# Strided sparse attention and an ELU layer pair: the order of the whole run written out as one list of small steps

## The chip, the cores and the metric

The kernel runs on one core of one Trainium2 chip. The metric is the device time of one execution in microseconds (us). The kernel before takes 330.32 us, the median of three runs (329.69 to 331.02).

Engines are named as in the profile: PE does matmuls, PEld is its loading of weights, DVE is VectorE, ACT is ScalarE, POOL is GpSimd, and SP is the sync engine, which here only issues DMAs. PSUM is eight banks of 128 x 512 fp32 that PE writes and DVE and ACT read.

## What is computed

Eight batches of eight heads, 576 rows of 64. Heads 0 to 3 look at the last 32 positions (local), heads 4 to 7 at all earlier positions with the same remainder by 32 (strided). The result, 4608 tokens of 512, goes through two weight matrices with an ELU between.

```python
scores = scale * np.matmul(q, k.transpose(0, 1, 3, 2))
mask_local = (rel >= 0) & (rel < stride)
mask_strided = (rel >= 0) & (pos[None, :] % stride == pos[:, None] % stride)
...
attn = attn / (np.sum(attn, axis=-1, keepdims=True) + 1e-09)
return np.matmul(attn, v).astype(np.float32)
...
h = x @ w_in
g = np.where(h > 0.0, h, alpha * (np.exp(np.minimum(h, 0.0)) - 1.0))
return (g @ w_out).astype(np.float32)
```

## The kernel before

**Tiling.** Each batch is four head pairs, called s0, s1 (strided) and l0, l1 (local). A pair's queries and keys are transposed so that the 64 features lie on partitions (lines 354 and 368 on PE for the early batches, lines 212 and 217 by DMA from SP for later ones: strided from batch 3, local from batch 4). Scores of keys by queries go to PSUM (line 451; line 479 for batch 0), ACT takes the exp (460 and 462; 488), DVE multiplies by a mask of zeros and ones (465; 495). Then PE multiplies by v, which has a column of ones for the denominator (515), DVE takes the reciprocal and normalises (522, 523) into x, PE transposes x (550, 563), and ACT or DVE copies it into xT (557, 559, 567), features by tokens. The local heads also need v of the 32 rows before each block, the halo (413).

**The two layers.** Tokens are taken in nine chunks of 512. For each of 16 column blocks of the first layer, `moe_in` does four matmuls (595), ACT takes exp (616), DVE computes min(e, 1) - 1 (623) and the max of that and h (625). For five blocks of the first chunk, ACT takes the Relu (619) and one DVE instruction does the rest (620). `moe_out` does a quarter of an output group of 128 tokens, four matmuls (635); after the fourth, ACT copies the bank out (639) and SP stores it (641).

**Order.** Nothing is scheduled by a tool: each engine runs its instructions in the order of the program. Batch 0 follows the list `OPENING`. From then on a loop over chunks alternates one `moe_in` of chunk nb with one `moe_out` of chunk nb - 1; in the 32 gaps between them stand pieces of the attention of batch nb + 1, at places set by `TIMES` (a start, a pitch from pair to pair, and the offset of each piece). A piece is coarse: `transposes` is the matmuls and the copy, `av` the matmuls and the normalisation, `scores_all` the scores of both halves of a pair, three exps and two masks.

**Banks.** A pair of neighbouring banks, `pair_a`, takes most of the scores of a pair; two single banks take the rest. Batch 0 has a second pair, `pair_b`, whose two banks serve the first layer later. The other single banks go round in small rings (`Ring`, `share`) for the first layer, the output groups, and everything else.

**Loads.** All loads of q, k, v and weights are DMAs from POOL, which cast fp32 to bf16, in the order of the program; only q of batch 0 is loaded as fp32 from SP and cast by ACT and DVE (341). Batch nb + 3 is loaded while chunk nb is computed, and the DMA transposes of batch nb + 2 are issued by `transpose_batch` at the seventh column block of chunk nb.

Of the kernel before, what the change touches and what calls it, by code (L numbers as in the profile page):

```python
# [10 lines left out]
F32 = mybir.dt.float32  # L11
# [7 lines left out]
STRIDE = 32  # L19
# [13 lines left out]
PIECES = (-2, -1, 0, 2, 3, 5, 7, 0)  # L33
TIMES = (
    None,
    (4, 6, (-3, -2, 0, 2, 4, 6, 9, 3)),
    (6, 6, (-3, -2, 0, 2, 4, 6, 8, 0)),
    (2, 7, PIECES),
)

OPENING = """
s0.cast_q s0.t_q s0.t_k s1.cast_q s1.t_k s0.s0 s1.t_q s0.s1 l0.t_q s1.s1 s1.s0 l0.t_k
l1.t_q l0.s0 s0.v l1.t_k s1.a0 s0.a0 l0.s1 s1.a1 s0.a1 l1.s0 l1.s1 s1.x s0.x s1.halo
l0.a0 l0.a1 l1.a0 l1.a1 l0.x moe.2 l1.x moe.3 moe.0 moe.1
""".split()
ON_VECTOR = "s0.t_q s1.cast_q s1.t_k l0.t_q s0.v l1.x".split()

MERGED = 1


ON_SCALAR = (4, 7, 10, 13, 15)
AHEAD = 3
# [3 lines left out]
def kernel(  # L59
# [24 lines left out]
    p_raw = inner.enter_context(tc.tile_pool(name="raw", bufs=2))  # L84
    p_p = inner.enter_context(tc.tile_pool(name="probs", bufs=3))
    p_x = inner.enter_context(tc.tile_pool(name="x", bufs=2))
    p_g = inner.enter_context(tc.tile_pool(name="g", bufs=2))


    ps = inner.enter_context(tc.tile_pool(name="ps", bufs=1, space=PSUM))  # L90
    pair_a = ps.tile([128, 2, 512], F32, tag="pair_a")
    singles = [ps.tile([128, 512], F32, tag=f"single{i}", name=f"single{i}")
               for i in range(4)]

    used = []

    class Ring:
        def __init__(self, *banks):
            self.banks = banks

        def next(self):

            for bank in self.banks:
                if all(bank is not u for u in used):
                    break
            else:
                bank = next(u for u in used if any(u is b for b in self.banks))
                used[:] = [u for u in used if u is not bank]
            used.append(bank)
            return bank  # L110


    rings = {}

    def share(sc, hps, ops, ring):
        rings.update(sc=Ring(*sc), hps=Ring(*hps), ops=Ring(*ops), ring=Ring(*ring))


    opening = ctx.enter_context(ExitStack())
    p_p0 = opening.enter_context(tc.tile_pool(name="probs0", bufs=8))  # L120
    p_k = opening.enter_context(tc.tile_pool(name="keys", bufs=1))
    ps_open = ctx.enter_context(ExitStack())
    ps_b = ps_open.enter_context(tc.tile_pool(name="ps_b", bufs=1, space=PSUM))
    pair_b = ps_b.tile([128, 2, 512], F32, tag="pair_b")

    def bf16_bank():
        return rings["ring"].next().bitcast(BF16)
# [11 lines left out]
    v_loc = [consts.tile([128, 4, 6, D + 1], BF16, tag=f"v_loc{i}", name=f"v_loc{i}")  # L139
             for i in range(3)]  # L140
    v_str = [consts.tile([128, 4, 5, D + 1], BF16, tag=f"v_str{i}", name=f"v_str{i}")
             for i in range(3)]

    def several(n, name, *shape):
        return [consts.tile([128, *shape], BF16, tag=f"{name}{i}", name=f"{name}{i}")
                for i in range(n)]
# [3 lines left out]
    nat = {(n, kind): several(3, f"{n}_{kind}", w * D)  # L150
           for n in "qk" for kind, w in (("str", 20), ("loc", 4 * L_RUN))}

    qT = {"str": several(2, "qT_str", 10, 128), "loc": several(2, "qT_loc", 2, 640)}
    kT = {"str": several(2, "kT_str", 10, 128), "loc": several(2, "kT_loc", 2, 32 + 640)}


# [5 lines left out]
    raw = {}  # L162
    src = {"q": q, "k": k, "v": v}

    def load_strided(b, name, engine=nc.gpsimd, heads=range(4)):
        rows = src[name][b, 4:8].rearrange("h (t r) d -> h t r d", r=STRIDE)
        if b == 0 and name in stage:
            t = stage[name]
        elif name == "v":
            if b not in raw:  # L170
                raw[b] = p_raw.tile([128, 4, 5, D], BF16, tag="v_raw", name="v_raw")
            t = raw[b]
        else:
            t = nat[name, "str"][b % 3].rearrange("p (h g d) -> p h g d", h=4, d=D)
        for h in heads:
# [32 lines left out]
    def transpose_batch(b):  # L208

        if b >= BY_DMA:  # L210
            for name, to in (("q", qT), ("k", kT)):
                nc.sync.dma_start_transpose(out=to["str"][b % 2],
                                            in_=nat[name, "str"][b % 3])
        if b >= EARLY:
            for name, to, o in (("q", qT, 0), ("k", kT, 32)):
                for a in range(2):
                    nc.sync.dma_start_transpose(
                        out=to["loc"][b % 2][:, a, o:o + 640].rearrange(
                            "p (i r) -> p i r", r=128),
                        in_=nat[name, "loc"][b % 3][:, 640 * a:640 * a + 640])  # L220

    def load_batch(b):
        for name in "qkv":
            load_strided(b, name)
        for name in "qkv":
            load_local(b, name)

# [16 lines left out]
    def clear_v(i, engine=nc.vector):  # L244
# [5 lines left out]
    share([pair_a, pair_b], [], [], singles[:3])  # L250
    warm = consts.tile([1, 1], F32, tag="warm")
    stage = {n: p_g.tile([128, 4, 5, D], F32, tag="g_sb", name=f"{n}_stage")
             for n in "q"}
# [10 lines left out]
    key_i = p_k.tile([128, 126], I32, tag="key_i")  # L264
# [4 lines left out]
    key_q = p_k.tile([128, 126], BF16, tag="key_q")  # L269
    nc.vector.tensor_copy(key_q, key_i)  # L270
    key_ps = bf16_bank()
    nc.tensor.transpose(key_ps[0:126, 0:126], key_q[0:126, :], identity[0:126, 0:126])
    diff = p_k.tile([128, 126], F32, tag="diff")
    same = p_k.tile([128, 126], F32, tag="same")
# [8 lines left out]
    for g in range(3):  # L283
        c = 252 + 108 * g
        nc.vector.tensor_copy(mask_s[0:126, c:c + 108], mask_s[0:126, 0:108])
    clear_v(0)
    nc.vector.memset(kT["loc"][0][:, :, 0:32], 0.0)

    load_strided(0, "k")
    load_local(0, "q")  # L290
    load_local(0, "k")
    load_strided(0, "v")

# [7 lines left out]
    load_local(0, "v")  # L301
# [3 lines left out]

    wi = moe_w_in.rearrange("(c p) f -> p c f", p=128)
    wo = moe_w_out.rearrange("(m p) d -> p m d", p=128)

    def load_w_in(i):
        nc.gpsimd.dma_start(out=w_in_sb[:, :, 512 * i:512 * (i + 1)],  # L310
                            in_=wi[:, :, 512 * i:512 * (i + 1)])

    load_w_in(0)
    load_strided(1, "q")
    load_strided(1, "k")
    load_w_in(1)
    load_strided(1, "v")
    load_local(1, "q")
    load_local(1, "k")
    load_w_in(2)  # L320


    class Pair:
        def __init__(self, b, strided, hp):
# [3 lines left out]
            self.name = f"{self.kind}{hp}"  # L328
            self.pr, self.x = {}, None

        def copy(self, step, late):

            if self.b == 0:
# [559 lines left out]
```

## Time and profile before

| What | us |
|---|---|
| median of three runs | 330.32 |
| profiled execution, its span | 330.3 |
| PE busy | 306.8 (93%) |
| DVE busy | 246.6 (75%) |
| ACT busy | 175.6 (53%) |
| POOL busy | 148.0 (45%) |
| first matmul of the first layer starts | 23.98 |
| first matmul of the second layer starts | 58.46 |
| last matmul ends | 324.70 |

The page of the profile also cuts the span into 40 slices of 8.26 us. Each digit below is the busy share of PE, of DVE and of the 16 DMA engines in tenths:

```
PE   0888778999999999999999999999999999999993
DVE  6583988788788888889889888888888666866500
DMA  6999999999999999999999906310001110010112
```

A busy PE is not PE at its peak: its matmuls overlap, and their ends are modelled. The distance from one start to the next tells the rate.

### The profile page before, as it was taken

The page shows a single profiled execution, that of the slowest core. Times are in us where ns is not written, and L with a number is a line of the kernel's source. Part 1 is how long each engine was busy: PE and PEld are TensorE (multiplying, and loading weights), DVE is VectorE, ACT ScalarE, POOL GpSimd, SP SyncE. Part 2 cuts the span into 40 slices and gives each one's busy share as a digit, 9 for nine tenths or more (in the row PEclk, how much of TensorE's full clock was granted, in tenths as well). Part 3 has the DMA queues.
Part 4 walks back from the last instruction along what each step waited for, and adds up shares of the span by engine and source line. Part 5 has one row for each costly group of instructions (what it writes and reads, how often), then busy time and mean ns, then how long its engine had stood idle before and what let it go on. Part 6 is the DMA issues. An engine that isn't in the chain of part 4 may idle for free.

```text
span 330.3 us, 6240 instructions
## 1 busy us (share of the span) xinstructions
PE 306.8 (93%) x2262; PEld 153.2 (46%) x2262; DVE 246.6 (75%) x540; ACT 175.6 (53%) x344; POOL 148.0 (45%) x233
## 2 busy tenths in 40 slices
PE   0888778999999999999999999999999999999993
PEld 0564444455545554454454444444444444444441
DVE  6583988788788888889889888888888666866500
ACT  3744968667555655554555455545664443444220
POOL 8988666996599479969796100000000000000000
PEclk9999979999999999999999999999999999999999
DMA  6999999999999999999999906310001110010112
GB/s 103 149 138 181 183 207 111 134 141 144 152 124 130 131 190 105 117 143 211 127 125 136 181 34 139 86 50 34 32 35 50 52 45 32 32 37 34 62 66 70
DMA packets 100092, 35.11 MB, mean 106 GB/s; under 512 B 77837, under 2 KB 95445, under 8 KB 100053
## 3 DMA queue, kind: packets, MB, share of 16 engines
q0 software_dynamic: 68016, 18.10, 59.7%
q1 hardware_dynamic: 32037, 16.52, 24.3%
q8 instruction: 20, 0.33, 0.4%
q14 instruction: 19, 0.16, 0.2%
HBM read 36.70 MB, written 9.44 MB: 140 GB/s over the span
## 4 chain that ended last, share of the span: by engine, by line
PE 81%; ACT 5%; DVE 5%; POOL 4%; issue 1%; DMA 1%; ACTq 0%; POOLq 0%
PE single L635 37%; PE half L595 32%; PE single L595 4%; PE single L515 3%; PE pair_a L451 1%; ACT e_sb L616 1%; ACT pr L462 1%; PE single L368 1%; DMA q_str<-in_q_dram 1%; DVE g_sb L625 1%; PE single L563 1%; PE single L550 1%; PE single L451 1%; DVE e_sb L623 1%; POOL v_loc L188 1%
## 5 line engine op out<-in xcount | busy, mean ns | idle before, releaser
L635 PE MATMUL single<-w_out_sb,g_sb 128*128 128x512 bf16 x576 | 145.5, 380 | 0.5
L595 PE MATMUL half<-xT,w_in_sb 128*128 128x512 bf16 x512 | 134.7, 385 | 0.5 <-DVE xT L567 0.5
L616 ACT ACTIVATE e_sb<-half 128x512 f32<-128x512 f32 x128 | 76.9, 600 | 99.8 <-PE half L595 97.0
L623 DVE TENSOR_SCALAR e_sb<-e_sb 128x512 bf16<-128x512 f32 x139 | 64.1, 461 | 44.8 <-ACT e_sb L616 42.7
L625 DVE TENSOR_TENSOR g_sb<-e_sb,half 128x512 bf16<-128x512 bf16 x123 | 84.6, 688 | 4.6
L635 PEld LDWEIGHTS <-g_sb 128*128 128x128 bf16 x576 | 53.5, 98 | 61.7 <-issue 2.5
L595 PEld LDWEIGHTS <-w_in_sb 128*128 128x128 bf16 x576 | 52.9, 100 | 57.0 <-issue 3.9
L639 ACT COPY o_sb<-single 128x512 f32<-128x512 f32 x36 | 21.3, 591 | 19.4 <-PE single L635 19.4
L515 PEld LDWEIGHTS <-pr 128*128 128x128 bf16 (+3 forms) x352 | 20.7, 106 | 16.6 <-issue 2.7
L462 ACT ACTIVATE pr<-pair_a 126x936 bf16<-126x936 f32 (+1 forms) x28 | 27.4, 979 | 0.0
L188 POOL DMA_DIRECT2D v_loc<-in_v_dram x32 | 24.5, 798 | 2.0 <-DMA k_loc<-in_k_dram 1.0
L176 POOL DMA_DIRECT2D k_str<-in_k_dram x32 | 21.2, 707 | 4.3 <-DMA w_out_sb<-in_moe_w_out_dram 2.3
L176 POOL DMA_DIRECT2D v_raw<-in_v_dram x32 | 22.2, 803 | 1.5 <-DMA k_str<-in_k_dram 0.9
L176 POOL DMA_DIRECT2D q_str<-in_q_dram x28 | 18.1, 660 | 10.4 <-DMA k_loc<-in_k_dram 5.2
L595 PE MATMUL single<-xT,w_in_sb 128*128 128x512 bf16 x64 | 18.7, 409 | 0.0
L523 DVE TENSOR_TENSOR x_l<-single,rden 96x384 bf16<-96x384 f32 x32 | 17.7, 553 | 1.1
L523 DVE TENSOR_TENSOR x_s<-single,rden 126x256 bf16<-126x256 f32 (+1 forms) x32 | 15.7, 491 | 1.1
L616 ACT ACTIVATE e_sb<-single 128x512 f32<-128x512 f32 x16 | 9.7, 609 | 11.0 <-PE single L595 11.0
L200 POOL DMA_DIRECT2D q_loc<-in_q_dram x16 | 12.9, 948 | 2.6 <-DMA v_raw<-in_v_dram 0.9
L460 ACT ACTIVATE pr<-single 108x108 bf16<-108x108 f32 (+1 forms) x56 | 11.3, 261 | 4.2 <-PE single L451 4.2
L465 DVE TENSOR_TENSOR pr<-pr,mask_l 128x192 bf16<-128x192 bf16 (+1 forms) x28 | 11.9, 452 | 2.0 <-ACT pr L462 1.9
L200 POOL DMA_DIRECT2D k_loc<-in_k_dram x16 | 12.1, 782 | 2.4 <-DMA q_loc<-in_q_dram 1.9
(106 smaller groups left out, 264.6 us busy)
## 6 DMA issues: line engine op xcount, KB each, us to landing
out_dram<-o_sb SPq DMA_DIRECT2D x36, 256.0 KB, 2.9
v_loc<-in_v_dram POOLq DMA_DIRECT2D x32, 72.0 KB, 5.8
k_str<-in_k_dram POOLq DMA_DIRECT2D x32, 67.5 KB, 4.3
v_raw<-in_v_dram POOLq DMA_DIRECT2D x32, 67.5 KB, 5.2
w_in_sb<-in_moe_w_in_dram POOLq DMA_DIRECT2D x4, 512.0 KB, 6.7
w_out_sb<-in_moe_w_out_dram POOLq DMA_DIRECT2D x4, 512.0 KB, 13.2
q_str<-in_q_dram POOLq DMA_DIRECT2D x28, 67.5 KB, 4.6
q_loc<-in_q_dram POOLq DMA_DIRECT2D x4, 288.0 KB, 5.6
```

The costliest lines, as they stand in the source:

```text
L176: engine.dma_start(out=t[0:108, h].rearrange("p g d -> p (g d)"), in_=rows[h, :, 0:30, :].rearrange("t (r g) d -> t r (g d)", g=5))
L188: nc.gpsimd.dma_start(out=v_loc[b % 3][32:128, h, :, :D], in_=v[b, h].rearrange("(i p) d -> p i d", p=LB))
L200: nc.gpsimd.dma_start(out=t[:, h // 2, 0:4, h % 2], in_=src[name][b, h, 0:512].rearrange("(i p) d -> p i d", p=128))
L462: nc.scalar.activation(main, sc[0:nk, :, 0:w], ACT.Exp, scale=scale)
L515: nc.tensor.matmul(av[0:m, p, blk - b0, :], lhsT=pr[0:nk, o:o + m], rhs=vt[0:nk, 2 * self.hp + p, blk, :], start=True, stop=True)
L523: nc.vector.tensor_tensor(self.x[0:nq, b0:b0 + n].rearrange("q g p d -> q p g d"), av[0:nq, :, 0:n, 0:D], r.unsqueeze(3).to_broadcast([nq, ...
L595: nc.tensor.matmul(hps, lhsT=w_in_sb[:, c, m * 128:(m + 1) * 128], rhs=xT[:, c, nb * N_TILE:(nb + 1) * N_TILE], start=start, stop=stop)
L616: nc.scalar.activation(e_sb, hps, ACT.Exp)
L623: nc.vector.tensor_scalar(e1_sb, e_sb, scalar1=1.0, scalar2=1.0, op0=ALU.min, op1=ALU.subtract)
L625: nc.vector.tensor_tensor(g_of[nb][:, m, :], e1_sb, hps, op=ALU.max)
L635: nc.tensor.matmul(ops, lhsT=g_of[nb][:, m, kk * 128:(kk + 1) * 128], rhs=w_out_sb[:, m, :], start=(m == 0), stop=(m == MC - 1))
L639: nc.scalar.copy(o_sb, ops)
```

## The change

`OPENING`, `PIECES`, `TIMES`, the rings and the loop over chunks are gone. In their place stands one list, `ORDER`, of about 1240 steps, and one loop that deals them out. A step names what is done, the bank or buffer that it uses (after @), and for copies the engine (after /: A is ACT, D is DVE, S a DMA from SP). Its first lines and a stretch from the steady part:

```diff
+ORDER = """
+0s0.cast/D 0s0.tq@1 0s1.cast/D 0s0.cq/A busy.1 0s1.tq@2 0s1.cq/D 0s0.tk@3 0s0.ck/D
+0s1.tk@4 busy.1 0s0.s1@0 0s1.ck/D 0s0.e1@0 0l0.tq@5 0s0.m1 0l1.tq@1 0l0.cq/A 0s1.s1@0
...
+5s1.s0@0 5s0.n1 o3.1.0@5 x4.4@2 5s1.halo 5s1.e0@2 i4.5@4 r4.4/D 5s1.m0 g4.4 5s0.x@6
```

Of a pair, tq and tk are the transposes on PE, cq and ck their copies, s0 and s1 the scores of the two halves, e the exp, m the mask, a the product with v, n the normalisation, x the transposes of x and y their copy, v the copies of strided v, halo the halo. Of the layers, i is an input group (i0.0.2 one matmul of it), x its exp, r the first part of the ELU, g the second, o a quarter of an output group, c its copy and store. What was one piece is now two or three steps that can stand apart.

What changes besides the order:

- **Banks.** One pair (slot 0) takes all scores, one half of a head pair at a time; the other six banks (slots 1 to 6) take everything else, each step naming its own.

```diff
+PAIRS = 1
-        def scores_all(self):
...
+        def s(self, u, copy, slot):
+            self.bank["s" + u] = sc = pairs_ps[slot]
...
+        def e(self, u, copy, slot):
+            if slot is not None:
+                self.pr = pr_sb[slot]
+            t, _, w = self.probs(int(u))
+            nc.scalar.activation(t, self.bank["s" + u][0:t.shape[0], :, 0:w], ACT.Exp,
+                                 scale=scale)
```

  Per head pair there are two exps of about 500 to 650 columns in place of two short and one long.

- **ELU.** The first part is written straight into g and the second works in place. Which column blocks take the Relu on ACT is in the list (r.../A): 11 of chunk 0, 26 of the chunks after it.

```diff
+        elif kind == "r":
+            e, by_scalar = e_of[c, i][0], copy == nc.scalar.copy
+            if by_scalar:
+                nc.scalar.activation(g[:, i, :], h_of[c, i], ACT.Relu)
+            else:
+                nc.vector.tensor_scalar(g[:, i, :], e, scalar1=1.0, scalar2=1.0,
+                                        op0=ALU.min, op1=ALU.subtract)
```

- **Fillers.** `busy(n)` is n matmuls of 512 columns on zeros into the last bank: 3 and 13 before batch 0, and 10 more in the opening of the list.

```diff
+    idle_sb = xT[:, 0, n_tokens - N_TILE:]
+    nc.gpsimd.memset(idle_sb, 0.0)
+
+    def busy(n):
+
+        for _ in range(n):
+            nc.tensor.matmul(singles[-1], lhsT=idle_sb[:, 0:128], rhs=idle_sb,
+                             start=True, stop=True)
```

- **Loads.** The order of POOL's loads up to batch 2 is a list, `LOADS`; local v of batch 0 comes before the selects that make the local mask. Strided v of batches 0 and 1 is loaded as fp32 from SP into the space of the second g buffer, and cast by the copies that place it.

```diff
+    stage = {"q0": staged[:, 0], "v0": staged[:, 1], "v1": staged[:, 1]}
...
+            load_strided(i, name, nc.sync if f"{name}{i}" in stage else nc.gpsimd)
```

- **DMA transposes.** They are steps of the list: turn.3s, turn.4s and turn.4l and so on, strided and local apart. turn.3s stands after c0.3 (the last store of chunk 0) and i2.0:

```diff
+o1.0.0@4 c0.3/A g1.15 2l1.x@1 o1.0.1 2l1.y/D i2.0@6 3s0.v0/D turn.3s 3s0.v1/D i2.1@5
+x2.0@2 i2.2@2 r2.0/D x2.1@0 g2.0 o1.0.2 r2.1/A x2.2@1 g2.1 i2.3@3 r2.2/D o1.0.3 g2.2
+x2.3@2 i2.4@1 r2.3/D c1.0/A g2.3 o1.1.0@6 x2.4@0 3s0.s0@0 r2.4/D i2.5@5 3s0.e0@0
```

The loop that deals the list out:

```diff
+    for token in ORDER:
+        token, _, slot = token.partition("@")
+        slot = int(slot) if slot else None
+        token, _, engine = token.partition("/")
+        copy = {"A": nc.scalar.copy, "S": None}.get(engine, nc.vector.tensor_copy)
+        what, _, rest = token.partition(".")
+        if what in pairs:
+            pairs[what].step(rest, copy, slot)
...
+        elif what == "turn":
+            (transpose_strided if rest[1] == "s" else transpose_local)(int(rest[0]))
+        elif what == "busy":
+            busy(int(rest))
         else:
+            moe(what[0], (what[1:], *rest.split(".")), copy, slot)
```

The numbers of matmuls, transposes, DMA transposes and stores of the computation itself are as before.

More of the change, by code (lines that the diff above doesn't have):

```diff
@@ L83, with several, bank, bank16 @@
     inner = ctx.enter_context(ExitStack())
[L84 to L87, printed above, removed]
+    work = inner.enter_context(tc.tile_pool(name="work", bufs=1))
     ps = inner.enter_context(tc.tile_pool(name="ps", bufs=1, space=PSUM))
[L91 to L127, printed above, removed]
+    def several(pool, n, name, *shape, dtype=BF16):
+        return [pool.tile([128, *shape], dtype, tag=f"{name}{i}", name=f"{name}{i}")
+                for i in range(n)]
+    pairs_ps = several(ps, PAIRS, "pair", 2, 512, dtype=F32)
+    singles = several(ps, 8 - 2 * PAIRS, "single", 512, dtype=F32)
+    def bank(i):
+        return pairs_ps[i][:, 0] if i < PAIRS else singles[i - PAIRS]
+    def bank16(i):
+        return (pairs_ps[i].bitcast(BF16)[:, 0] if i < PAIRS
+                else singles[i - PAIRS].bitcast(BF16))
     w_in_sb = consts.tile([128, KC, d_ff], BF16, tag="w_in_sb")
@@ L304 @@
     nc.vector.memset(kT["loc"][1][:, :, 0:32], 0.0)
[L306 to L320, printed above, removed]
+    for what in LOADS[LOADS.index("w.in.0"):]:
+        load(what)
     class Pair:
@@ L440, in scores_all, with v @@
[L440 to L447 removed]
+        def v(self, part, copy, slot):
+            o = rows_of(v_str[self.b % 3][:, :, :, 0:D], slice(0, 4))[int(part)]
+            copy(o, rows_of(strided_dst(self.b, "v"), slice(0, 4))[int(part)])
@@ L467, in scores_all @@
[L467 to L479 removed]
+                nc.tensor.matmul(sc[:, half, i * nq:(i + 1) * nq],
```

643 lines of the change are left out of this document (310 added, 333 removed).

## The prediction, made before the changed kernel was run

> **What bounds the kernel now.** I read the busy times by stage first, then what PE waits for, then PE's own timeline in the opening. The stages are cut at PE's first transpose of q (7.91), its first input-layer matmul (23.98), the first ELU exp (29.03), the first output-layer matmul (58.46) and PE's last matmul (324.70). Columns: busy us of PE, PEld, DVE, ACT, POOL, then granted clock, DMA, GB/s.
>
> ```profile
> 0.00:7.91 7.91, 0.37 (x2) 0.19 (x2) 5.27 (x24) 2.36 (x5) 6.89 (x18) 1.00 0.60 99
> 7.91:23.98 16.07, 13.35 (x172) 9.78 (x173) 11.28 (x30) 9.65 (x18) 14.55 (x23) 1.00 1.25 146
> 23.98:29.03 5.05, 5.05 (x20) 2.14 (x18) 1.35 (x4) 0.64 (x1) 4.22 (x8) 1.00 1.15 160
> 29.03:58.46 29.43, 22.68 (x237) 12.87 (x236) 24.31 (x52) 24.34 (x49) 20.76 (x32) 0.94 1.24 168
> 58.46:324.70 266.24, 265.31 (x1838) 128.25 (x1836) 204.41 (x432) 137.99 (x271) 101.55 (x157) 1.00 0.79 97
> 324.70:330.30 5.60, 0.01 (x1) 0.00 (x0) 0.00 (x0) 0.59 (x1) 0.00 (x0) 0.95 0.16 54
> ```
>
> From 58.46 on PE is busy 265.31 of 266.24 us and DVE 77%. All waits of PE from 58 to 325 are one line:
>
> ```profile
> PE half L595 <- DVE xT L567: 0.5, 1, 0.5
> ```
>
> So nothing is to be won there except fewer matmuls, and the change removes none; it can only lose there. What can be won lies before 58.46, where no engine is full. There the first twelve input matmuls (two, one, two, one ...) run at half rate:
>
> ```profile
> 27.02 1.06 PE L595 MATMUL half<-xT,w_in_sb 128*128 128x512 bf16 x2
> 27.87 0.63 PE L595 MATMUL single<-xT,w_in_sb 128*128 128x512 bf16 x1
> 28.30 1.06 PE L595 MATMUL half<-xT,w_in_sb 128*128 128x512 bf16 x2
> ...
> 31.65 1.04 PE L595 MATMUL half<-xT,w_in_sb 128*128 128x512 bf16 x4
> ```
>
> Three take 28.30 - 27.02 = 1.28, 0.427 each; at 31.65 four take 0.87 up to the next start (32.52), 0.217 each. The stage costs 5.05 where 12 x 0.215 = 2.6 would do.
>
> **Steady part and tail: 266.24 + 1.1 + 5.60.** The output layer, its copies and the last store are the same steps, so the tail stays 5.60. At the first output matmul the old order has already done one input group of the next chunk (four matmuls from 57.35, 0.86) and the last transposes of batch 1 (0.21); the new list has them still to do: +1.1. Shorter exps on ACT (two of 0.59 to 0.72 a pair for 0.27 + 0.27 + 0.98) and Relus moved to ACT for 26 column blocks after the first chunk's cost nothing, for both engines have room under PE; without that room each Relu would cost 0.61 on ACT.
>
> **Opening to the first input group: 27.1 in place of 29.03.** Two filler groups (3 and 13 matmuls on zeros) run while PE waits for q, from 3.65 to 7.91 in the old trace; sixteen at 0.427 are 6.8, so from about 2 they end near 9 at worst, before the cast below. The casts of q both go to DVE; the second waits for q's last two heads, as in the old trace at 9.69. From there DVE has, up to the last strided copy into xT: casts, q and k copies, eight masks, eight normalisations, the halo, v. At the mean durations of their rows that is 15.5 us. Means overlap: the 52 DVE instructions of the old stage 29.03 to 58.46 have durations that add to 26.7 against 24.31 busy, so 0.91: 14.2. Waits on the way, worked along the list: second half of q, the copy before the second mask, v by SP's queue: 1.6. End 9.7 + 14.2 + 1.6 = 25.5; the first group's first bank is done seven matmuls later, 1.5 warm: 27.0, exp at 27.1. Bounds: 26 (no waits) and 29.5 (one us for v, matmuls at 0.427).
>
> v of batches 0 and 1 leaves POOL's queue for SP's: ten issues of 0.8 less on POOL, which lets the local v and the weights be issued 3 us earlier; on SP they stand behind q's five, which end at 4.87, so the first five end near 9, as they did on POOL (9.70), and share the transfer engines with k. Hence the one us above.
>
> Eight score steps now share one pair of banks, where the opening had two pairs. Each is matmuls 0.25, exp 0.65 and handover 0.1, so 8 x 1.0 = 8 us in a row, inside DVE's 14.2; if DVE were faster, this would be next.
>
> **First exp to the first output matmul: 23 in place of 29.43.** In this stretch the list gives DVE 13 final ELU steps x 0.69, 5 first halves x 0.45, 8 masks (3.6), 7 normalisations (4.9), five copies (2.7), the halo (0.5): 23.0; and ACT 15 exps x 0.60, 9 Relus x 0.61, 8 score exps (5.2), five copies (3.3): 23.0. Times 0.91 each is 20.9. The old order was busy 24.31 of 29.43 on DVE. Walking the list with these durations, DVE and ACT seldom find their next step unready, since scores, ELU blocks and copies alternate; I allow 2 us of waits: 22.9. Bounds: 20.9 (none) and 20.9 x 29.43 / 24.31 = 25.3 (as loose as before). First output matmul: 27.1 + 22.9 = 50.0, bounds 47 to 55. There PE waits 0.3 for the last normalisation of batch 1.
>
> Weights cover this: the output weights' transfers are issued by 39.42, a median of 13.2 us before they land, so the last is there at about 52; the list needs the first two at 50 to 51 and the third only after four other groups, about 56. DMA is full through this stage, so if they came 4 us later PE would stop here.
>
> **The new wait: 3 us.** Strided q and k of batch 3 are transposed by DMA from SP's queue. The old order issued that a chunk and a half ahead:
>
> ```profile
> 69.83 1.63 SPq L212 DMA_TRANSPOSE qT_str<-q_str  x1
> 73.62 1.77 SPq L212 DMA_TRANSPOSE kT_str<-k_str  x1
> 75.49 26.58 SPq L641 DMA_DIRECT2D out_dram<-o_sb  x4
> ```
>
> The answer on that tile gives issue to landing:
>
> ```profile
> DMA to landing us min/median/max: 3.4/9.9/10.7
> ```
>
> 3.4 is the last batch, when little else moves. In the new list this pair stands behind the store of chunk 0's last 128 rows on SP. From the first output matmul to the last for that store PE has 16 output and 16 input groups (32 x 0.863 = 27.6) and batch 2's transposes, scores and value products (6.5): 34.1; its copy ends 0.7 later, its store is issued by 35.4; q's transpose takes SP to 37.4, and k's lands 9.9 later, at 47.3. PE wants it ten groups on, after 43.0 of steps; the same sum of steps gives 260.5 for the old 266.24, so 43.9. All is behind it, in PE's order. Wait 3.4; with 3.4 to landing (40.8) none; with 10.7, 4.2. I take 3, since loads of batch 4 are then under way, as in the rows near 10. Later batches have 12 us and more between the queue's turn and their scores, and the four DMA transposes of x stand 8.3 us and more ahead of their chunk against 5.8 to landing, so they are hidden.
>
> **Sum.** 50.0 + 0.3 + 266.24 + 1.1 + 5.6 + 3 = 326.2; say 326. The profiled execution spans 330.3 and the median of the runs is 330.32, so no correction between them.
>
> **A rule against it.** The old trace shows 0.427 per matmul after 16 us of transposes and small matmuls and 0.215 after 5 us of full ones. The Trainium skill (TensorE: Matmul & The Clock Gate, Part 4: PE-mode transpose) says that transposes do not count as PE work for the gate; this trace agrees that they left it cold. By that rule the fillers ahead would be forgotten by the time of the first input group; what it would cost is the third rival, from rows.
>
> **The rivals.**
> 1. No transpose wait and a tight opening: 47 to 50 + 273.2 = 320.5 to 323.3. For it: 3.4 to landing has been seen, and a list can have been set by such times. Against: four of five k transposes are near 10.
> 2. The opening is shorter and it is given back: opening at 52 to 53, wait 4, and small waits in the steady part: 53 + 273.2 + 4 = 330.2. For it: both DVE and ACT must be nearly full for 23 us. Against: their work, 21, leaves room.
> 3. PE is cold again when the first input groups come: 9 matmuls x 0.212 = 1.9 later, and 1 more after the transpose wait (in the old trace a clock of 0.83 at 40 to 50 follows gaps of 1.45 and 1.26, at 34.41 and 43.17): 329.
> 4. Slower, by the pair of score banks. The old steady order used it once per head pair, 6.9 to 8 us apart; the new one uses it twice, and between the two stand 1.4 to 1.9 us of PE steps in most pairs. In that time ACT must finish an ELU exp that stands ahead (0.5) and the score exp (0.65), with handovers 0.2: 1.35. It decides from where ACT is 0.3 late: there PE loses what ACT is late, about 30 times. At 0.6 late, 30 x 0.3 = 9: 335. For it: PE is strictly in order, and ACT's Relus are more. Against: ACT is busy 52% in the steady part.
>
> Each engine's built order follows the list, so that the change does nothing is ruled out.
>
> **Chances.** Forecast (324 to 328.5) 0.37; rival 1 0.25; rival 2 0.12; rival 3 0.10; rival 4 0.16. A measurement here tells about 0.5%, 1.65 us, from no change: faster is below 328.7, slower above 332.0. Faster: 0.35 + 0.25 + 0.06 + 0.01 = 0.67; same: 0.02 + 0.08 + 0.04 = 0.14; slower: 0.03 + 0.16 = 0.19. Range: from the tight opening, 319.5, to the light end of rival 4, 333.
>
> **What would show it.** In the new profile: first 512-column input matmuls 0.215 apart and the first exp at about 27; first output matmul at 50; one wait of PE for k's transpose of batch 3, near 93; no other wait of PE above 0.5 in the steady part; tail 5.6. Waits of PE on score exps in every pair would prove rival 4; a first output matmul after 54 would prove my opening wrong.

## The result and the profile after

The changed kernel takes 332.78 us (median of 6 runs, 331.49 to 333.02) against 330.0 for the kernel before beside it (329.15 to 331.02): ratio 1.0075, interval 1.0052 to 1.0099. It is slower by 0.5 to 1.0%. The profiled execution spans 331.2.

The table of stretches of the changed kernel, cut at the same events as the old one: first transposes of q, first input matmul, first ELU exp, first output matmul, PE's last matmul. Columns: busy us of PE, PEld, DVE, ACT, POOL, then granted clock, DMA, GB/s.

```profile
8.30:25.24 16.94, 11.37 (x165) 6.97 (x166) 11.29 (x25) 7.81 (x14) 10.86 (x18) 0.80 1.31 170
25.24:31.61 6.37, 5.45 (x50) 2.94 (x47) 5.26 (x16) 1.56 (x3) 5.27 (x7) 1.00 1.16 184
31.61:53.01 21.40, 19.64 (x217) 10.47 (x216) 20.34 (x47) 19.90 (x38) 10.79 (x17) 1.00 1.39 191
53.01:325.15 272.14, 270.63 (x1848) 128.88 (x1846) 203.61 (x429) 147.36 (x259) 106.14 (x165) 1.00 0.78 97
325.15:331.20 6.05, 0.01 (x1) 0.00 (x0) 0.00 (x0) 0.59 (x1) 0.00 (x0) 0.89 0.15 50
```

The first ELU exp comes later than before (31.61 for 29.03), the first output matmul earlier (53.01 for 58.46): the opening gained 5.45. The steady part lost more than that: 272.14 for 266.24, with PE still busy 99% of it. PE's waits in it, as listed for 53 to 326, are one line in place of the old one:

```profile
PE pair L489 <- DMA kT_str<-k_str: 1.5, 1, 1.5
```

So a wait explains a quarter of the 5.9; the rest is time in which PE counts as busy. PE's timeline shows where. A head pair's scores in the new kernel (start, us from first to last, line, shapes, count; a start-to-start difference is the time a step really took):

```profile
173.10 1.03 PE L633 MATMUL single<-w_out_sb,g_sb 128*128 128x512 bf16 x4
174.06 0.30 PE L489 MATMUL pair<-qT_loc,kT_loc 64*128 64x96 bf16 x6
174.30 1.04 PE L607 MATMUL single<-xT,w_in_sb 128*128 128x512 bf16 x4
175.17 1.03 PE L633 MATMUL single<-w_out_sb,g_sb 128*128 128x512 bf16 x4
176.03 0.42 PE L553 MATMUL single<-identity,x_s 126*128 126x126 bf16 x5
176.39 0.30 PE L489 MATMUL pair<-qT_loc,kT_loc 64*128 64x96 bf16 x6
176.62 1.04 PE L607 MATMUL single<-xT,w_in_sb 128*128 128x512 bf16 x4
```

and in the kernel before:

```profile
174.13 1.03 PE L635 MATMUL single<-w_out_sb,g_sb 128*128 128x512 bf16 x4
175.09 0.22 PE L451 MATMUL single<-qT_loc,kT_loc 64*128 64x96 bf16 x2
175.15 0.38 PE L451 MATMUL pair_a<-qT_loc,kT_loc 64*128 64x96 bf16 x10
175.46 1.04 PE L595 MATMUL half<-xT,w_in_sb 128*128 128x512 bf16 x4
176.33 0.42 PE L550 MATMUL single<-identity,x_s 126*128 126x126 bf16 x5
176.59 1.03 PE L635 MATMUL single<-w_out_sb,g_sb 128*128 128x512 bf16 x4
```

Four full-width matmuls take 0.86 up to another full-width step (172.03 to 172.89 in the new trace), but 0.96 up to a score step (173.10 to 174.06): 0.10 for going in. From the last score matmul to the next full-width one are 0.14, where small steps of full height leave some 0.04: 0.10 for coming out. The old kernel's twelve score matmuls cost 175.46 - 174.13 - 0.86 = 0.47; the new kernel's two stretches of six cost (174.30 - 173.10 - 0.86) + (176.62 - 176.03 - 0.26) = 0.34 + 0.33 = 0.67. That is 0.20 more per head pair, and batches 2 to 7 have 24 pairs in the steady part: 4.8 us. The Trainium skill has the rule for it (TensorEngine Tiling (Array Packing), Key Properties): changing the tiling mode, not just the tile, drains TensorE. Both traces agree, with 0.2 a visit.

The scores are the only matmuls here on 64 rows. PE's transposes of local q and k, on 96 rows but 64 columns, show the same price, as here in the kernel before:

```profile
72.92 0.42 PE L550 MATMUL single<-identity,x_s 126*128 126x126 bf16 x5
73.27 0.45 PE L368 MATMUL single<-identity,q_loc 96*64 96x96 bf16 x12
73.65 1.04 PE L635 MATMUL single<-w_out_sb,g_sb 128*128 128x512 bf16 x4
```

Five transposes of x take 73.27 - 72.92 = 0.35 ahead of them, and 0.26 ahead of a full-width step (176.33 to 176.59 above); the last transpose of local q is 0.14 ahead of the next full-width matmul. So it is the change of shape that costs, by rows or by columns.

What made the first exp late is at the start of the opening. The chain that ends at it, in order of time (start, us, what):

```profile
5.90 10.73 DMA k_loc<-in_k_dram
16.64 0.04 issue
16.68 1.17 PE single L435 x24
17.85 0.32 PE pair L489 x2
18.18 0.97 PE single L366 x2
```

Local k lands at 16.64, while DVE stands waiting for its transposes (start, us, line, shapes, and in brackets the idle time before):

```profile
13.25 0.50 DVE L516 TENSOR_TENSOR pr<-pr,mask_s 108x648 bf16<-108x648 bf16 x1 [0.77 <-ACT pr L505]
14.71 0.76 DVE L450 COPY qT_loc<-single 128x576 bf16<-128x576 bf16 x1 [0.97 <-PE single L435]
15.74 0.50 DVE L516 TENSOR_TENSOR pr<-pr,mask_s 108x648 bf16<-108x648 bf16 x1 [0.27 <-ACT pr L505]
17.89 0.76 DVE L450 COPY kT_loc<-single 128x576 bf16<-128x576 bf16 x1 [1.65 <-PE single L435]
```

In the kernel before, local q and k were issued at about the same time and landed at 10.94 and 12.72; here at 13.93 and 16.64.

### The profile page after: what moved, and what is told of

It reads as the page before. It is cut to its first block, busy times and chain, and to the rows that moved or that the text cites. A ratio compares the mean times of both kernels' runs of the same rounds, so it can differ in the third digit from the quotient of the medians.

```text
span 331.2 us, 6254 instructions
## 1 busy us (share of the span) xinstructions
PE 312.7 (94%) x2288; PEld 151.2 (46%) x2288; DVE 246.3 (74%) x540; ACT 179.1 (54%) x316; POOL 140.7 (42%) x224
## 4 chain that ended last, share of the span: by engine, by line
PE 83%; DVE 6%; DMA 5%; ACT 2%; POOL 2%; issue 0%; DVEq 0%; ACTq 0%; POOLq 0%
PE single L633 37%; PE single L607 35%; PE pair L489 4%; PE single L530 3%; DMA k_loc<-in_k_dram 3%; DMA kT_str<-k_str 2%; PE single L435 1%; DVE x_l L542 1%; PE single L553 1%; DVE pr L516 1%; DVE g_sb L624 1%; POOL k_str L257 1%; ACT pr L505 1%; PE single L559 1%; ACT e_sb L612 1%; DVE x_s L542 1%
## 5 line engine op out<-in xcount | busy, mean ns | idle before, releaser
L607 PE MATMUL single<-xT,w_in_sb 128*128 128x512 bf16 x576 | 147.1, 380 | 0.3 <-DVE xT L579 0.3
L612 ACT ACTIVATE e_sb<-single 128x512 f32<-128x512 f32 x144 | 86.1, 601 | 100.4 <-PE single L607 91.4
L618 DVE TENSOR_SCALAR g_sb<-e_sb 128x512 bf16<-128x512 f32 x107 | 49.4, 462 | 37.1 <-ACT e_sb L612 35.3
L627 DVE TENSOR_TENSOR g_sb<-g_sb,single 128x512 bf16<-128x512 bf16 x107 | 73.3, 685 | 2.9
L505 ACT ACTIVATE pr<-pair 128x576 bf16<-128x576 f32 (+2 forms) x64 | 42.0, 656 | 12.4 <-PE pair L489 12.3
L624 DVE SCALAR_TENSOR_TENSOR g_sb<-e_sb,g_sb 128x512 bf16<-128x512 f32 x37 | 25.4, 688 | 2.9 <-ACT g_sb L616 1.0
L616 ACT ACTIVATE g_sb<-single 128x512 bf16<-128x512 f32 x37 | 22.2, 601 | 0.0
L516 DVE TENSOR_TENSOR pr<-pr,mask_l 128x576 bf16<-128x576 bf16 x32 | 14.5, 453 | 4.9 <-ACT pr L505 4.8
L542 DVE TENSOR_TENSOR x_s<-single,rden 108x384 bf16<-108x384 f32 (+1 forms) x32 | 15.7, 491 | 1.1
L516 DVE TENSOR_TENSOR pr<-pr,mask_s 108x648 bf16<-108x648 bf16 (+1 forms) x32 | 14.5, 453 | 1.7 <-ACT pr L505 1.3
```

The lines of the kernel that those rows point to most:

```text
L505: nc.scalar.activation(t, self.bank["s" + u][0:t.shape[0], :, 0:w], ACT.Exp, scale=scale)
L516: nc.vector.tensor_tensor(t, t, mask.unsqueeze(1).to_broadcast([nk, 2, w]), op=ALU.mult)
L542: nc.vector.tensor_tensor(self.x[0:nq, b0:b0 + n].rearrange("q g p d -> q p g d"), av[0:nq, :, 0:n, 0:D], r.unsqueeze(3).to_broadcast([nq, ...
L607: nc.tensor.matmul(h_of[c, i], lhsT=w_in_sb[:, cc, i * 128:(i + 1) * 128], rhs=xT[:, cc, c * N_TILE:(c + 1) * N_TILE], start=j == 0, stop= ...
L612: nc.scalar.activation(e_sb[slot], h_of[c, i], ACT.Exp)
L618: nc.vector.tensor_scalar(g[:, i, :], e, scalar1=1.0, scalar2=1.0, op0=ALU.min, op1=ALU.subtract)
```

## The experiments

All times stand beside runs of the kernel before on the same chip (medians 329.4 to 330.0). Spans are those of single profiled executions. In the changed kernel and its variants such an execution's time is 1.8 us above its span (333.02 and 331.2; 331.56 and 329.7), and so it is in the runs of the kernel before beside them (329.28 and 327.4); so two spans are compared with each other, not with a median.

### The DMA wait

The token that issues batch 3's two transposes goes ahead of the store that held SP's queue.

```diff
-... c0.3/A g1.15 ... 3s0.v0/D turn.3s 3s0.v1/D
+... c0.2/A turn.3s g1.11 ... c0.3/A g1.15 ... 3s0.v0/D 3s0.v1/D
```

> The changed kernel with the DMA transposes of batch 3's strided q and k issued ahead of the store of chunk 0's last 128 rows but one (right after its third output copy). Theory: PE's wait for kT_str at about 95, 1.6 us start to start, goes and nothing takes its place: 1.6 us less, 331.2. Rival: the transposes then lie among batch 4's loads and the stores and end as late as before, or the next step is late instead: no change, 332.8.

Measured: 330.49 us (12 runs), ratio 1.0001 (0.9979 to 1.0023). SP's queue in the changed kernel, then in this one:

```profile
81.01 8.77 SPq L641 DMA_DIRECT2D out_dram<-o_sb  x2
90.07 2.27 SPq L291 DMA_TRANSPOSE qT_str<-q_str  x1
92.58 2.18 SPq L291 DMA_TRANSPOSE kT_str<-k_str  x1
```

```profile
81.35 0.33 SPq L638 DMA_DIRECT2D out_dram<-o_sb  x1
81.99 1.87 SPq L288 DMA_TRANSPOSE qT_str<-q_str  x1
84.10 2.21 SPq L288 DMA_TRANSPOSE kT_str<-k_str  x1
```

The queue reaches the transposes 8 us earlier and PE's wait is gone. The gain, 2.3, is above the 1.6 that the trace showed, but the two intervals leave room for 1.4 to 3.5; in the profiled execution, the longest of the twelve, the stretch from the first output matmul to PE's last is only 0.8 shorter (271.33 for 272.14). PE's wait in the changed kernel, from 97.7 to 99.2, is not one number either: in the other runs that kept the old place it was 0.8, 1.0, 2.8, 3.5 and 4.0, and what a long one costs besides is told in the last section.

### The price of a stretch of score matmuls, doubled in the kernel before

The last four score matmuls of each pair of batches 4 to 7 are issued one gap earlier, so that there are two stretches a pair and everything else stays.

```diff
+    self.score_mms(self.places()[0][-4:], [self.sc[:, 0], self.sc[:, 1]])
...
+    self.score_mms(found[:-4] if self.b >= 4 else found, banks)
...
+                               (at[2] - 1, pr.scores_first),
                                (at[2], pr.scores_all if b >= MERGED
```

> The kernel before with the score matmuls of the 16 pairs of batches 4 to 7 in two stretches instead of one: the last four matmuls of the stretch are issued one gap earlier, into the same banks; exps, masks and everything else stay. Theory: 16 more stretches of 64-row matmuls cost 0.2 us each, 3.2 us more: 333.2 against 330.0. Rival: going into and out of 64-row matmuls costs nothing that other work doesn't hide: within 0.5 us of 330.0.

Measured: 334.0 us, ratio 1.013 (1.0097 to 1.0163), 4.05 more for 16 stretches: 0.25 each, 0.20 to 0.34 by the interval. In the profiled executions the stretch from the first output matmul to PE's last is 269.85 for 266.24, 0.23 each. The second stretch has a price that nothing hides, on the old kernel with its own order.

### The two score steps made one again in the changed kernel

First all of a pair's score matmuls in one step (S: ten or twelve matmuls into the pair and two singles; E: three exps; M0 and M1: two masks), as before the change, in 23 pairs:

```diff
-4s1.s0@0 i3.5@4 r3.4/D 4s1.e0@2 g3.4 4s0.x@5 4s1.m0 4s1.s1@0 x3.5@2 o2.1.1 4s0.y/D 4s1.e1
+4s1.S@4+6 i3.5@5 r3.4/D 4s1.E@2 g3.4 4s0.x@2 4s1.M0 x3.5@2 o2.1.1 4s0.y/D
-r3.5/D i3.6@3 g3.5 4s1.m1 4s1.a0@2
+r3.5/D i3.6@4 g3.5 4s1.M1 4s1.a0@6
```

> The changed kernel with the two score steps of a head pair made one again in 23 of the 24 pairs of batches 2 to 7 (all matmuls in one stretch into the pair and two free single banks, three exps and two masks, as in the kernel before). Theory: each stretch of 64-row score matmuls costs PE about 0.2 us besides its matmuls, 0.096 going in and 0.10 coming out; 23 stretches fewer are 4.6 us less, 328.2, all of it in the stretch from the first output matmul to PE's last. Rival: the extra 5.9 us of that stretch come from PE waiting on ACT and DVE in the hand-made order, whatever the number of stretches; then the longer exps (1.52 for 1.3 a pair) gain nothing or lose up to 2 us: 332.5 to 335.

Measured: 332.65 us. In some pairs the list has the first value product ahead of the second mask, so part of these products read unmasked probabilities. It gained nothing. PE's waits of its steady part:

```profile
PE single L518 <- DMA kT_str<-k_str: 4.0, 1, 4.0
PE single L586 <- DVE pr L545: 3.0, 5, 0.9
```

If 23 stretches fewer saved 4.6, an estimate at 0.20 each, more than that was put back: on the list 3.0 for masks that come late behind longer exps and 2.5 more at the DMA wait, and in the profiled execution, the longest of the six, the steady part is 276.45, 4.3 more than without the edit. The next run is meant to remove both: transposes earlier, the step one column block earlier, both masks ahead of the value product, in 20 pairs.

```diff
-i3.4@6 c2.0/A 4s1.halo 4s0.n1 o2.1.0@1 x3.4@1 turn.5s g3.3 4s1.s0@0 i3.5@4 r3.4/D 4s1.e0@2
+i3.4@1 c2.0/A 4s1.halo 4s0.n1 4s1.S@3+6 o2.1.0@5 4s1.E@2 x3.4@1 turn.5s g3.3 i3.5@2 r3.4/D
```

> The changed kernel with batch 3's DMA transposes issued earlier (330.5 by itself) and one score step a pair in the 20 pairs of batches 3 to 7, this time one column block earlier in PE's order and with both masks ahead of the first value product. Theory: 20 stretches of 64-row matmuls fewer, 0.2 to 0.25 us each, 4 to 5 us less than 330.5: 325.5 to 326.5, and no new wait of PE. Rival: the longer exps make the masks late and PE waits for them instead, as in the run with 23 pairs merged (3.0 us in five places): 329 to 330.5.

Measured: 342.75 us, 12.3 more than the run with the transposes alone. My edit made a new wait:

```profile
PE single L586 <- DVE pr L545: 12.7, 17, 2.3
```

With 1.5 us of exps in one piece on ACT the ELU exps behind them come late, DVE stands at its next ELU step, in order (45.9 us in all for such exps, 35.3 in the changed kernel), and the mask behind that is late for PE. This list was dealt for two short exps; a long one in it costs more than two stretches.

So the third form leaves exps, masks and products where they are, and only puts the second stretch right behind the first, into two more banks. A first try made these from halves of pair tiles:

```diff
-singles = several(ps, 8 - 2 * PAIRS, "single", 512, dtype=F32)
+pairs_ps = several(ps, 4, "pair", 2, 512, dtype=F32)
+singles = [p[:, h] for p in pairs_ps[1:] for h in range(2)]
```

> The changed kernel with batch 3's DMA transposes earlier (330.5 by itself) and, in the 16 pairs of batches 4 to 7, the second score step's matmuls put right behind the first's, into a second pair of banks made of two that are free; exps, masks, value products and their order stay as they are. Theory: 16 stretches of 64-row matmuls fewer at 0.20 to 0.25 us: 3.2 to 4.0 less, 326.5 to 327.3, with no wait of PE on masks. Rival: the price is not one of going in and out of 64-row matmuls, or PE waits for the banks instead: 330 or more.

Measured: 379.9 us. Its first two PE waits:

```profile
PE pair L629 <- DVE g_sb L623: 17.9, 22, 1.5
PE pair L603 <- ACT e_sb L608: 3.9, 7, 1.1
```

Output matmuls (L629) waited for ELU steps, which read another bank: halves of one tile seem to be waited for as one, which I infer from such pairs and did not test by itself. The run says nothing of the stretches. The same with two separate singles, and two exps of one bank each at the old place of the second:

```diff
-4s1.s0@0 i3.5@4 r3.4/D 4s1.e0@2 g3.4 4s0.x@5 4s1.m0 4s1.s1@0 x3.5@2 o2.1.1 4s0.y/D 4s1.e1
+4s1.s0@0 4s1.s1@3+4 i3.5@5 r3.4/D 4s1.e0@2 g3.4 4s0.x@1 4s1.m0 x3.5@2 o2.1.1 4s0.y/D 4s1.e1
```

> The changed kernel with batch 3's DMA transposes earlier (330.5 by itself) and, in the 16 pairs of batches 4 to 7, the second score step's matmuls right behind the first's, this time into two free single banks, so that nothing couples the banks of the ELU blocks; its exp is then two of one bank each at the old place, about 0.3 us more of ACT a pair. Theory: 16 stretches of 64-row matmuls fewer at 0.20 to 0.25 us: 3.2 to 4.0 less, 326.5 to 327.3, no wait of PE on exps or masks above 0.5. Rival: what the stretches save comes back as waits for masks, as in both runs with one merged step: 329.5 or more.

Measured: 327.4 us (325.68 to 327.88), ratio 0.9896 (0.9861 to 0.9931): 3.1 less than with the transposes alone, for 16 stretches, 0.19 each, 0.13 to 0.30 by the two intervals. PE's timeline of one pair:

```profile
218.63 1.03 PE L611 MATMUL single<-xT,w_in_sb 128*128 128x512 bf16 x4
219.50 1.03 PE L637 MATMUL single<-w_out_sb,g_sb 128*128 128x512 bf16 x4
220.45 0.28 PE L488 MATMUL pair<-qT_str,kT_str 64*128 64x126 bf16 x4
220.57 0.31 PE L488 MATMUL single<-qT_str,kT_str 64*128 64x108 bf16 x6
220.81 1.04 PE L611 MATMUL single<-xT,w_in_sb 128*128 128x512 bf16 x4
```

220.81 - 219.50 - 0.86 = 0.45 for ten score matmuls, one way in and one way out, and no wait of PE above 0.3 in that stretch. The steady part takes 267.2 from its first output matmul to the last. This version is faster than both kernels.

### What made the opening late

Four runs put v back to POOL's queue, all of it or in part, in bf16. In the first, batch 2's v went into the buffer of batch 0's ahead of its copy, so the value products of batch 0 are made with another batch's v.

```diff
-stage = {"q0": staged[:, 0], "v0": staged[:, 1], "v1": staged[:, 1]}
+stage = {"q0": staged[:, 0]}
```

> The changed kernel with the strided v of batches 0 and 1 loaded from POOL's queue in bf16, as the kernel before did, in place of SP's queue in fp32. Theory: the fp32 loads of v, issued at 4.9 to 9.9 on SP, share the transfer engines with the local q and k and delay them; without them local q lands near 11 and local k near 13 (13.9 and 16.6 in the changed kernel), PE's waits for them (1.5 and 1.8) and most of that for v_loc go, the first ELU exp comes at 28.0 to 29.5 in place of 31.6, and the time is 2 to 3 us less, 330 to 331. Rival: DVE's chain, or the single pair of score banks, sets the opening; the local loads land earlier but the first exp stays within 0.5 of 31.6 and the time at 332.8.

Measured: 374.95 us, with 45.6 of PE's wait at that copy; it tells nothing of the question. The second gives each v a place of its own (staged_v is bf16):

```diff
-stage = {"q0": staged[:, 0], "v0": staged[:, 1], "v1": staged[:, 1]}
+stage = {"q0": staged[:, 0], "v0": staged_v[:, 0], "v1": staged_v[:, 1]}
-load_strided(i, name, nc.sync if f"{name}{i}" in stage else nc.gpsimd)
+load_strided(i, name, nc.gpsimd)
```

> The changed kernel with the strided v of batches 0 and 1 loaded in bf16 from POOL's queue in place of fp32 from SP's, each into a place of its own. Theory: as stated for the run before it: local q lands near 11 and local k near 13, the first ELU exp comes at 28.0 to 29.5 in place of 31.6, and the time is 2 to 3 us less than the changed kernel's 332.8: 330 to 331. Rival: DVE's chain or the single pair of score banks sets the opening: the first exp stays within 0.5 of 31.6 and the time at 332.8.

Measured: 340.83 us. Local q and k landed at 11.5 and 13.1 and the first input matmul came at 22.55 (25.24), as expected; then DVE came to the copy of batch 1's v:

```profile
25.87 0.42 DVE L541 TENSOR_TENSOR x_s<-single,rden 126x256 bf16<-126x256 f32 x1
33.44 0.36 DVE L475 COPY v_str<-g_sb 108x768 bf16<-108x768 bf16 x1 [7.15 <-DMA g_sb<-in_v_dram]
```

On POOL's queue that v is behind two quarters of the input weights; this is what SP's queue was good for. The third moves batch 0's v alone:

```diff
-load_strided(i, name, nc.sync if f"{name}{i}" in stage else nc.gpsimd)
+load_strided(i, name, nc.sync if f"{name}{i}" == "v1" else nc.gpsimd)
```

> The changed kernel with only batch 0's strided v loaded in bf16 from POOL's queue; batch 1's stays on SP where the change put it (with both moved, DVE stood 6.7 us at the copy of batch 1's v). Theory: fp32 v of batch 0 on SP's queue delays the local q and k; without it the first full group of input matmuls starts near 22.6, as in the run with both moved (25.2 in the changed kernel), nothing stops DVE, the first ELU exp comes at 28.5 to 29.5 and the time is 2 to 3 us less than 332.8: 330 to 331. Rival: ELU blocks and the rest of DVE's chain then set the first output matmul, which stays at 52.5 to 53; the time stays within 0.7 of 332.8.

Measured: 337.44 us. The first full input matmuls stayed at 25.0 and the first exp at 31.1: local k landed at 14.9, and what POOL issued behind v came later (first input weights at 24.55 for 21.62). The edit did more than its description says. In the changed kernel both v share one buffer, so SP issues batch 1's only from 19.35 on; with batch 0's out of it, SP issues batch 1's fp32 v from 4.92 on, and local k has fp32 v beside it as before. So the run does not test the theory. The first output matmul stayed at 52.91, as the rival says, but its time fails too: the transposes of batch 3 were waited for 2.8, and the steady part of the profiled execution is 3.6 longer (275.73). A fourth run takes both v to POOL and moves batch 1's two copies down to the steps that need them, with the transposes early:

```diff
-0s1.n0 1s0.v0/A 0l1.x@5 1s0.v1/D 0s1.x@1
+0s1.n0 0l1.x@5 0s1.x@1
...
-i0.5@2 1s0.e1 r0.3/D 1s0.a0@3 x0.4@1 1s1.s0@0 1s0.m1
+i0.5@2 1s0.v0/A 1s0.e1 r0.3/D 1s0.a0@3 x0.4@1 1s1.s0@0 1s0.v1/D 1s0.m1
```

> The changed kernel with the transposes earlier (330.5 by itself), both strided v of batches 0 and 1 loaded in bf16 from POOL's queue, and the two copies of batch 1's v moved in ACT's and DVE's order to just ahead of the steps that need them, so that DVE does not stand 6.7 us at them as it did where they were. Theory: with local q and k landed by 11.5 and 13.1 the opening is shorter by the 2.6 us of DVE waits for them: first ELU exp at 28.5 to 29.5 (31.6), and 2 to 2.5 us less in the end, 328 to 328.5. Rival: the weights and batch 1's loads, 3 to 5 us later on POOL's queue, hold PE or DVE instead: 331 or more.

Measured: 330.5 us (12 runs), ratio 1.0018 (0.9992 to 1.0045), against 330.49 without the v edit. The loads and the first exp are as the theory says: k's issue to landing

```profile
k_loc<-in_k_dram POOLq DMA_DIRECT2D x1, 288.0 KB, 6.8
```

for 10.7 in the changed kernel, first exp at 29.18 for 32.08. So v's fp32 loads on SP's queue did make the local q and k late, by 2.7 and 3.9 us (landed at 11.24 for 13.93 and 12.71 for 16.64). But nothing of it shows in the time, though the two intervals leave room for about 1 us. The first output matmul came 1.4 earlier in this execution (51.20 for 52.60). A likely reason for the loss of the other half, not tested by itself: the two copies now lie behind the first exp, in a stage where DVE is busy 20.28 of 22.02 and ACT 20.41 (19.48 and 19.76 of 20.52 without). The remaining 1.4 is less than such executions differ by (328.8 to 332.2).

Without the filler matmuls:

```diff
 def busy(n):
-    for _ in range(n):
+    for _ in range(0):
```

> The changed kernel without its filler matmuls on zeros (16 ahead of the list and 10 in it). Theory: they cover waits of PE for q, k and v and keep the granted clock no better than 0.80 before 25; without them the first full-width matmuls run at most 1 us slower in all, and the ends of other steps move by less than 1 us: 332 to 333.8. Rival: they are what warms PE; without them all of PE's work up to 50 runs at half rate and the time is 2 us or more above 332.8.

Measured: 333.72 us, ratio 1.0118 (1.0080 to 1.0156), not told apart from the changed kernel. First exp at 31.68 for 31.61. Two fillers lie on the chain above (0.97 at 18.18), and what fillers cost they bring back in PE's pace. Without them:

```profile
24.43 1.04 PE L607 MATMUL single<-xT,w_in_sb 128*128 128x512 bf16 x2
25.27 0.69 PE L559 MATMUL single<-identity,x_l 96*128 96x96 bf16 x6
...
29.14 2.93 PE L607 MATMUL single<-xT,w_in_sb 128*128 128x512 bf16 x9
31.91 0.71 PE L429 MATMUL single<-identity,k_str 126*128 126x126 bf16 x10
```

The first two input matmuls take 0.42 each (0.22 in the changed kernel, at 25.24), and the nine ahead of the first exp start earlier (29.14 for 29.90) but take 2.77 in place of 1.94. So the rival is right that they warm PE, and wrong on what that is worth.

### Everything together

Three runs put edits from above together. The first: both v on POOL's queue, the transposes early, one score step a pair as in e7_turn_merge.

> The changed kernel with all three edits: v from POOL's queue in bf16, batch 3's DMA transposes earlier, and one score step a pair in batches 3 to 7. Theory: the three gains are in different stretches and add: 332.8 - 2.5 - 2.3 - 4.3 = 323.7, below both kernels. Rival: a shorter opening meets later weights or the DMA transposes again, and part of it is given back: 326 to 328.

Measured: 349.38 us. The second: batch 0's v on POOL's queue and e8_adjacent.

> The two edits above together: v of batch 0 from POOL's queue, transposes of batch 3 earlier, score steps side by side in batches 4 to 7. Theory: gains in different stretches, they add: 330.5 - 3.6 - 2.5 = 324.4, below both kernels. Rival: batch 0's earlier end is given back before the first output matmul: 326.5 to 327.3.

Measured: 379.3 us. Both carry the faults of their parts, late masks and batch 1's v in the one, the halves of tiles and batch 1's early fp32 loads in the other, and show nothing more. The third: e10_side and e11_v_late.

> The two edits above in one kernel. Theory: different stretches, they add: 330.5 - 3.6 - 2.2 = 324.7. Rival: the opening's part is given back at batch 1's later loads: as the run with the score steps alone, 326.5 to 327.3, or more.

Measured: 328.25 us (12 runs), ratio 0.9942 (0.9913 to 0.9971). It does not add. The interval overlaps that of e10_side alone, so the opening's edit shows no gain there either.

## Why the prediction was wrong

The sum was 50.0 + 0.3 + 266.24 + 1.1 + 3 + 5.6 = 326.2 by spans; the span is 331.2. Of the 5.0 between them 3.0 lie ahead of the first output matmul (53.01 for 50.0), 1.5 from there to PE's last matmul (272.14 for 270.64) and 0.45 in the tail (6.05 for 5.60; in the variants it runs from 5.1 to 6.1). Two steps failed, and the second of these numbers is small only because errors offset each other.

**Steady part: the first step that failed.** "It can only lose there" was right, but the loss was put at 1.1 (one input group and transposes left over) and the wait. The term for the split of the scores held ACT's shorter exps, which it put at nothing, and not what a visit to 64-row matmuls costs PE. It is 0.20 a pair in the traces, 24 times: 4.8. Doubling it in the old kernel cost 0.25 each, undoing it in the new one brought 0.19. The old trace had the price, 0.096 ahead of every score step. The parts add to 1.1 + 1.6 + 4.8 = 7.5 for a loss of 5.9. By start-to-start times, 1.2 of the difference are gaps between input and output matmuls in the old steady part that the new one does not have, and 0.6 is the old kernel's own wait of PE (0.5 on its list). Another 0.4 is saved where a stretch of scores runs straight into transposes of local q or k, four times, with one change of shape in place of two. That leaves 5.3; the other 0.6 stays open. The forecast also met the 2% between its own sum of steps (260.5) and the old 266.24 and took it for a pace.

**Rival 2 had the course and not the cause.** An opening that ends at 52 to 53 and is given back is what happened (53.01), but it was to be given back in waits, 4 of them for the transposes, and not in the steps themselves.

**Rival 4 had the place and not the mechanism.** It saw the score steps of a pair twice as often, and priced ACT's lateness at the single pair of banks. PE's list of waits has no line for it.

**Opening to the first exp, the second step that failed: 27.1, measured 31.61.** The terms that failed are DVE's waits, 1.6, and less so its work, 14.2. From its cast of q's last two heads (9.57) to the last strided copy into xT (29.85) DVE took 20.3: 5.3 idle, 15.0 busy. The forecast saw that v on SP's queue shares the transfer engines, and charged one us to v; it was the local q and k, behind it in need but beside it in the queues, that paid 3.0 and 3.9. The e11_v_late run got 2.9 back. The remaining 2.1 above the forecast are in that run too: DVE waits 1.88 for a value product of strided heads (24.68), which in PE's order stands behind the first input matmuls, whose weights landed at 22.05, and three fillers. But the item is smaller than it looks, since in the end that run gained nothing.

**First exp to first output: 22.9, measured 21.40.** Right, with its reason: DVE busy 20.34 and ACT 19.90, work sums against 20.9, and 1 to 1.5 of waits. The first output matmul, 53.01, lies in the bounds 47 to 55. Weights were covered, as said.

**The new wait: 3, measured 1.5.** Place and cause were right; e2_turn_early shows it. PE comes to it at 97.7, for near 93 in the forecast, 3.0 of that from the later opening. The size varies from 0.8 to 4.0 between the runs that kept the old place, so both 3 and 1.5 are sizes that it takes.

**Rival 3.** The nine input matmuls ahead of the first exp, 29.90 to 31.84, took 0.216 each: PE was warm, with fillers between the transposes. Without them (e5_no_fill) it was cold behind 16 us of transposes and small matmuls, 0.42 a matmul at 24.43, which agrees with the Trainium skill's rule on transposes (TensorE: Matmul & The Clock Gate, Part 4: PE-mode transpose). The clock column reads 1.00 there, as in the old kernel's row from 23.98 to 29.03 beside 0.427 a matmul, so the openings are read by the spacing. But it decided nothing in the time: the first exp came at the same time, for without fillers PE reached the nine matmuls 0.76 earlier.

**Time and span.** "No correction between them" does not hold. With 1.8 between time and span, as in the runs above, the old profiled execution would be one of 332.1, an estimate, 2.1 above its median. So the two spans differ by 0.9 and the medians by 2.8; where the old kernel's other executions are shorter, no trace here shows.

## What to carry to other kernels

Count visits, not only matmuls: where PE sets the end, each stretch of matmuls of another shape (here 64 rows, or 64 columns) has a price of its own, read from start-to-start times at its two edges, and work of that kind belongs together; "busy" hides it. An order dealt by hand for each engine holds what it was dealt for: an edit that lengthens one step (1.5 us of exps) stops engines that have half their time free, so that an experiment on it has to leave the lengths alone. And a load taken off one queue is not gone: ask which loads in flight share the engines with it, and which stand behind it now.

## What the runs showed of the hardware

- Going from full-height matmuls to 64-row ones and back costs PE 0.10 and 0.10 us, alike in every kernel here (medians 0.311 or 0.312 for 0.216 ahead of a score step; 0.135 to 0.141 behind it, where other small steps leave 0.03 to 0.05). Transposes with 64 columns cost the same (0.308 or 0.309 ahead of them, 0.138 or 0.139 behind).
- A long wait of PE costs more than itself. After one of 3.54 us, which ends at 101.22, the granted clock falls and matmuls run at half rate, in the run without fillers:

```profile
96.00:100.00 4.00, 1.68 (x8) 0.59 (x6) 2.75 (x5) 1.18 (x2) 2.88 (x5) 1.00 1.88 155
100.00:104.00 4.00, 2.78 (x14) 0.98 (x16) 1.24 (x3) 1.19 (x2) 3.60 (x7) 0.82 1.81 158
104.00:108.00 4.00, 4.00 (x42) 2.01 (x42) 2.32 (x6) 1.90 (x3) 4.00 (x8) 0.76 0.96 101
```

  By start-to-start times about 1.4 us went that way there (0.41 to 0.43 a matmul from 102.5 on, for 0.216), and about 1.6 in the runs with waits of 4.0 and 2.8; behind the 1.5 of the changed kernel nothing did. The Trainium skill puts the gate's idle window at some 3.4 us (TensorE: Matmul & The Clock Gate, Part 1); 3.54 and 4.0 agree, and 2.8 was enough as well. In the openings, with small matmuls between, shorter waits stand ahead of such a stretch: the granted clock is 0.50 from 18 to 22 in the changed kernel, behind waits of 1.51 and 1.76, and from 43.1 to 46.4 in the old one, around waits of 0.48 and 1.26.
- Loads on SP's queue slow those of POOL's: 288 KB of local k took 10.7 us from issue to landing beside 576 KB of fp32 v on SP, 6.8 without, and 9.0 in e1c_v0_pool beside batch 1's. The Trainium skill says that all queues run on the same 16 engines and interleave (Trainium Kernel Development and Optimization, Key Constraints); this is its size here.
